# A convolution and spectral mixing kernel: the first row block through another queue, taps and masks on 32 partitions

## Chip, cores and metric

The kernel runs on one core of a Trainium2 chip. A core has TensorE (PE: matrix products, results in PSUM), VectorE (DVE), ScalarE (ACT), GpSimd (POOL) and SyncE (SP), each with its own instruction queue, and 16 DMA engines which carry out the transfers that SP, ACT and POOL issue. The metric is the time of one execution in microseconds (us). The three runs before lie between 171.89 and 172.04, with a median of 171.96.

## What is computed

The input `x` is (8, 3264, 192) in float32: batch, sequence, channels. The first step is a causal convolution along the sequence with 7 taps for each of 8 heads of 24 channels; the taps are a softmax of `weight` (8, 7). The second step works on the result: a Fourier transform along the sequence, of which 64 modes are kept and multiplied by complex 192 x 192 matrices, transformed back and added.

```python
w = np.exp(weight - np.max(weight, axis=-1, keepdims=True))
w = w / (np.sum(w, axis=-1, keepdims=True) + 1e-09)
...
out = np.einsum('hk,bskhg->bshg', w, x_unf)         # causal, 7 taps, group of 24 channels
...
X = np.fft.rfft(x, axis=1)
Xr, Xi = (np.real(X[:, :n_modes]), np.imag(X[:, :n_modes]))
Yr = np.einsum('bmd,mde->bme', Xr, w_r) - np.einsum('bmd,mde->bme', Xi, w_i)
Yi = np.einsum('bmd,mde->bme', Xr, w_i) + np.einsum('bmd,mde->bme', Xi, w_r)
Y[:, :n_modes] = Yr + 1j * Yi
u = x + np.fft.irfft(Y, n=S, axis=1)
return (u + np.maximum(u @ w_ch, 0.0)).astype(np.float32)
```

## The kernel before

The sequence is cut into 13 row blocks of 256 rows (the last has 192), the batches into four pairs. `xall` holds all of `x` in bf16: one partition holds two neighbouring rows (a row pair) of one block, side by side for both batches of a pair. Slot 0 of `xall` is zero, as the past of the first block; of the last block of each pair only 96 partitions are filled by loads, and the other 32 (the tails) are set to zero. The order of the instructions on each engine is that of the program text.

**Loads.** All of `x` comes on POOL's queue (q0), in transfers that read float32 and write bf16. Six units of 5, 8, 9, 10, 10 and 10 blocks (`UNITS`) are loaded by `load_unit`, one transfer for each batch of a pair (L165) and one for the short last block (L169). Behind them, on the same queue, come the 64 mode matrices `moe_w_r` and `moe_w_i` (L296), into `arena` and into the end of `ct`. A new transfer waits until the transfer eight places before it has landed. SP's queue carries only `weight` at the start (L172) and all outputs at the end (L691).

**Band.** The convolution is a product with a band matrix. VectorE builds it: the softmax taps (L224 to L234), four masks (L199) that compare an index `cidx` with 0 to 3, and 14 predicated copies (L242) that put taps into `packed` where a mask holds. Until now this was done on all 128 partitions, with `goff` (L188) and L197 correcting `cidx` in each group of 32. Four small copies for each half of the heads (ScalarE L250, VectorE L252) then bring `packed` into `band`. Before that ScalarE writes zeros into the band (L186) and into the tails (L190).

**Convolution and tables.** TensorE first runs 92 idle matmuls (L196), then convolves unit by unit (L317); ScalarE and VectorE copy the results back into `xall` (L351, L353, L359, L361). The sine and cosine tables are computed beside that (L209 to L221), and the transform along the sequence is a product with them (L378). Between the units, and after them, TensorE transposes `xall` into `ct` (L419).

**Mixing and output.** L551 multiplies four modes at a time, in 16 groups, each with matrices from q0. The last group is followed by the output stage: L723 and L703 form the products of the channel matrix and of the inverse transform, ScalarE clamps (L696), VectorE adds (L685) and SP stores (L691).

The lines of the table builder and the order of the load and the idle matmuls are in the functions printed below.

Of the kernel before, what the change touches and what calls it, by code (L numbers as in the profile page):

```python
# [9 lines left out]
ALU = mybir.AluOpType  # L10
ACT = mybir.ActivationFunctionType
AX = mybir.AxisListType
F32 = mybir.dt.float32
# [7 lines left out]
def kernel(  # L21
# [9 lines left out]
    nc = tc.nc  # L31
    B, S, D = x.shape
    H, KK = weight.shape
# [4 lines left out]
    P = 128  # L38
    NQ = B // 2
    NB = S // (2 * P) + 1  # L40
    NT = 2 * NB
    PL = (S - 2 * P * (NB - 1)) // 2
    NSLOT = NQ * NT + 2
    PW = 32 + KK // 2
# [10 lines left out]
    def sb(name, shape, dtype):  # L55
        return pool.tile([P] + shape, dtype, tag=name, name=name)
# [7 lines left out]
    ct = sb("ct", [NQ * NT * 3, P], BF16)  # L64
# [7 lines left out]
    band = shared[:, 0:H * 2 * BW].rearrange("p (h o c) -> p h o c", h=H, o=2)  # L72
# [7 lines left out]
    ascale = sb("ascale", [1], F32)  # L80
    halfpi = sb("halfpi", [1], F32)
    xs = [sb(f"xs{i}", [2, D], BF16) for i in range(2)]
    xacc = ct[:, 0:6, :].rearrange("p t s -> p (t s)").bitcast(F32)
    ylate = xs[0][:, :, :].rearrange("p i d -> p (i d)")


    xin = xall[:, :, :, :].rearrange("p (b x) i d -> p b (x i d)", x=2)
# [15 lines left out]
    def temp(n, dtype):  # L103
        w = n * 2 if dtype == F32 else n
        a = arena[:, pos[0]:pos[0] + w]
        pos[0] += (w + 15) // 16 * 16
        return a.bitcast(dtype) if dtype != BF16 else a
# [5 lines left out]
    wsub = temp(H * KK, F32)  # L113
    wexp = temp(H * KK, F32)
    taps = temp(H * KK, BF16)
    wmax = temp(H, F32)
    wsum = temp(H, F32)
    wrec = temp(H, F32)
    wsin = temp(H, F32)
    cidx = temp(PW, F32)  # L120
    goff = temp(1, F32)
    masks = temp((KK // 2 + 1) * PW, U16)
    sidx = temp(NT, F32)
    midx = temp(MODES, F32)
# [30 lines left out]
    def load_unit(g0, n):  # L155
        for part in parts_of(g0, n):
            load_part(*part)

    def load_part(q, b0, n):
        nf = min(n, NB - 1 - b0)  # L160
        s0 = NB * q + b0 + 1
        for i in range(2):
            off = ((2 * q + i) * S + 2 * P * b0) * D
            src = bass.AP(tensor=x.tensor, offset=x.offset + off, ap=[[2 * D, P], [2 * P * D, nf], [1, 2 * D]])
            nc.gpsimd.dma_start(out=xin[:, s0:s0 + nf, 2 * D * i:2 * D * (i + 1)], in_=src)  # L165
        if nf < n:
            off = (2 * q * S + 2 * P * (NB - 1)) * D
            src = bass.AP(tensor=x.tensor, offset=x.offset + off, ap=[[2 * D, PL], [S * D, 2], [1, 2 * D]])
            nc.gpsimd.dma_start(out=xin[0:PL, s0 + nf, :].rearrange("p (i c) -> p i c", i=2), in_=src)  # L169

    wr3 = wraw.rearrange("p (h k) -> p h k", h=H)
    nc.sync.dma_start(out=wr3, in_=bass.AP(tensor=weight.tensor, offset=weight.offset,  # L172
                                           ap=[[0, P], [KK, H], [1, KK]]))
    load_unit(*units[0])
    nc.gpsimd.iota(cidx[:, 0:PW], pattern=[[1, PW]], base=0, channel_multiplier=-1,
                   allow_small_or_imprecise_dtypes=True)
    load_unit(*units[1])
    nc.gpsimd.iota(sidx.rearrange("p (b a) -> p b a", a=2), pattern=[[2 * P, NB], [1, 2]], base=0,
                   channel_multiplier=2, allow_small_or_imprecise_dtypes=True)
# [4 lines left out]
    zero = packed[:, 0:2].bitcast(F32)  # L184
    bandrow = shared[:, 0:H * 2 * BW].bitcast(F32)
    nc.scalar.copy(out=bandrow, in_=zero.to_broadcast([P, H * BW]))  # L186
    for g in range(4):
        nc.vector.memset(goff[32 * g:32 * g + 32, :], float(32 * g))  # L188
    tails = xin[PL:P, NB:NB * NQ + 1:NB, :].bitcast(F32)
    nc.scalar.copy(out=tails, in_=zero[PL:P, :].unsqueeze(2).to_broadcast([P - PL, NQ, 2 * D]))  # L190
    nc.vector.memset(halfpi[:], math.pi / 2)
    nc.vector.memset(ascale[:], 2.0 / S)
    nc.vector.memset(ascale[0:2 * B, :], 1.0 / S)
    zeros = xall[:, 0, 0, :]
    for _ in range(NIDLE):
        nc.tensor.matmul(free[3][:, 0, 0:144], zeros[:, 0:P], zeros[:, 0:144], start=True, stop=True, skip_group_check=True)  # L196
    nc.vector.tensor_scalar(out=cidx[:, 0:PW], in0=cidx[:, 0:PW], scalar1=goff[:, 0:1], scalar2=None, op0=ALU.add)  # L197
    for k in range(KK // 2 + 1):
        nc.vector.tensor_scalar(out=masks[:, PW * k:PW * (k + 1)], in0=cidx[:, 0:PW],  # L199
                                scalar1=float(k), scalar2=None, op0=ALU.is_equal)  # L200
    tu3 = turns.rearrange("p (t m) -> p t m", t=NT)
    wh3 = whole.rearrange("p (t m) -> p t m", t=NT)
# [1 line left out]
    def table(step, t0, t1):  # L204
# [15 lines left out]
        else:  # L220
            nc.scalar.activation(out=ftab[:, t0:t1, 0:2 * MODES - 1:2], in_=wh, func=ACT.Sin, scale=-TWOPI,  # L221
                                 bias=halfpi[:, 0:1])

    nc.vector.reduce_max(out=wmax, in_=wr3, axis=AX.X)  # L224
    nc.vector.tensor_tensor(out=wsub.rearrange("p (h k) -> p h k", h=H), in0=wr3,
                            in1=wmax.unsqueeze(2).to_broadcast([P, H, KK]), op=ALU.subtract)
    nc.scalar.activation(out=wexp, in_=wsub, func=ACT.Exp)
    nc.scalar.activation(out=wsin, in_=ascale.to_broadcast([P, H]), func=ACT.Sin)
    we3 = wexp.rearrange("p (h k) -> p h k", h=H)
    nc.vector.reduce_sum(out=wsum, in_=we3, axis=AX.X)  # L230
    nc.vector.tensor_scalar(out=wsum, in0=wsum, scalar1=1e-9, scalar2=None, op0=ALU.add)
    nc.vector.reciprocal(out=wrec, in_=wsum)
    ta3 = taps.rearrange("p (h k) -> p h k", h=H)
    nc.vector.tensor_tensor(out=ta3, in0=we3, in1=wrec.unsqueeze(2).to_broadcast([P, H, KK]), op=ALU.mult)  # L234


    pk4 = packed.rearrange("p (h o c) -> p h o c", h=H, o=2)
    for h0 in (0, H // 2):
        hs = slice(h0, h0 + H // 2)
        for lag in range(KK):  # L240
            k = lag // 2
            nc.vector.copy_predicated(  # L242
                out=pk4[:, hs, lag % 2, :],
                mask=masks[:, PW * k:PW * (k + 1)].unsqueeze(1).to_broadcast([P, H // 2, PW]),
                data=ta3[:, hs, KK - 1 - lag:KK - lag].to_broadcast([P, H // 2, PW]))
        for g in range(4):
            c0 = 1 + 32 * (g % 2)
            dst, srcv = band[32 * g:32 * g + 32, hs, :, c0:c0 + PW], pk4[32 * g:32 * g + 32, hs, :, :]
            if h0 == 0:
                nc.scalar.copy(out=dst, in_=srcv)  # L250
            else:
                nc.vector.tensor_copy(out=dst, in_=srcv)  # L252
# [4 lines left out]
                            base=0, pattern=[[-1, P]], channel_multiplier=1)  # L257
    nc.gpsimd.memset(perm[:], 0.0)
    nc.gpsimd.affine_select(out=perm[:, 0:64], in_=perm[:, 0:64], compare_op=ALU.not_equal, fill=-1.0,
                            base=-64, pattern=[[-1, 64]], channel_multiplier=1)  # L260
    nc.gpsimd.affine_select(out=perm[:, 64:128], in_=perm[:, 64:128], compare_op=ALU.not_equal, fill=1.0,
                            base=0, pattern=[[-1, 64]], channel_multiplier=1)

    for i in range(2):
        nc.gpsimd.memset(apart[i][:], 0.0)
        for c in range(2):
            nc.gpsimd.affine_select(out=apart[i][:, 64 * c:64 * c + 64], in_=apart[i][:, 64 * c:64 * c + 64],
                                    compare_op=ALU.not_equal, fill=-1.0 if (i, c) == (1, 0) else 1.0,
                                    base=-(c ^ i), pattern=[[-2, 64]], channel_multiplier=1)
# [601 lines left out]
```

## Time and profile before

| | |
|---|---|
| median of three runs | 171.96 us |
| the profiled execution, its whole time | 171.92 us |
| its span, first to last instruction | 169.8 us |
| TensorE (matmul) busy | 160.1 us, 94% |
| VectorE busy | 125.7 us, 74% |
| ScalarE busy | 109.8 us, 65% |
| GpSimd busy | 44.3 us, 26% |
| POOL's queue q0 | 19.62 MB |
| SP's queue q1 | 20.09 MB |

The profile shows one execution. Besides the span there are 2.1 us around it. The page gives busy time by engine, then the span in 40 slices of 4.245 us with a digit for the busy tenths of each, then the chain of waits that ended last, followed back from the last instruction, and groups of instructions by line. The trace answers more closely: the chain in order of time, instructions by time (the timeline), and busy time in windows that one names. Lines like L551 are lines of the kernel before; in the changed kernel the same code lies eight lines lower from the convolution on.

### The profile page before, as it was taken

What the parts mean: (1) busy time and instruction counts of PE and PEld (TensorE: products, weight loads), DVE (VectorE), ACT (ScalarE), POOL (GpSimd) and SP (SyncE); (2) the same over time, 40 slices, a digit from 0 to 9 for tenths busy, and PEclk for the clock granted to TensorE, in tenths of its full rate; (3) what the DMA queues carried; (4) which work ended last, traced back from release to release, by engine and by line L of the source; (5) the groups of instructions that cost most, each with busy time, mean ns of one, the idle gap of its engine ahead of it and who ended that gap; (6) DMA issues with size and microseconds to landing.
All of it is one profiled execution on the core that took longest, in us unless ns stands there. A gap on an engine that the chain in (4) does not pass through costs nothing.

```text
span 169.8 us, 6332 instructions
## 1 busy us (share of the span) xinstructions
PE 160.1 (94%) x2643; PEld 129.9 (77%) x2643; DVE 125.7 (74%) x245; ACT 109.8 (65%) x209; POOL 44.3 (26%) x81
## 2 busy tenths in 40 slices
PE   6996999999999999999999889999999999999990
PEld 6983776775655656589999655899899999999960
DVE  4899762883763846568778544899899999999990
ACT  8485870753663627447677554688788888888771
POOL 7941963522521612003520000990000000000000
PEclk9999999999999999999999999999999999999999
DMA  3999999999999999999999970588989989999996
GB/s 28 201 203 203 204 205 203 204 204 204 201 205 204 209 205 208 208 208 208 209 204 209 208 120 4 192 299 321 365 333 346 350 300 358 358 324 339 330 343 221
DMA packets 36956, 40.10 MB, mean 236 GB/s; under 512 B 2272, under 2 KB 36928, under 8 KB 36928
## 3 DMA queue, kind: packets, MB, share of 16 engines
q0 software_dynamic: 22624, 19.62, 72.1%
q1 hardware_dynamic: 14304, 20.09, 32.3%
q8 instruction: 20, 0.33, 0.8%
q14 instruction: 8, 0.07, 0.1%
HBM read 39.10 MB, written 20.05 MB: 348 GB/s over the span
## 4 chain that ended last, share of the span: by engine, by line
DMA 57%; PE 37%; issue 1%; POOL 1%; ACT 1%; POOLq 0%
PE z L723 34%; DMA xall<-in_x_dram 25%; DMA arena<-in_moe_w_i_dram 18%; DMA ct<-in_moe_w_i_dram 14%; PE z L703 1%; POOL xall L165 1%; PE z L644 0%; PE z L551 0%; ACT z L696 0%; ACT arena L683 0%; PE z L635 0%; ACT shared L569 0%; PE z L645 0%; PE z L575 0%; PE z L804 0%
## 5 line engine op out<-in xcount | busy, mean ns | idle before, releaser
L685 DVE TENSOR_TENSOR arena<-z,xall 128x384 f32<-128x384 f32 (+1 forms) x103 | 57.0, 557 | 3.0 <-PE z L723 1.2
L696 ACT ACTIVATE z<-z 128x384 f32<-128x384 f32 x102 | 48.1, 475 | 12.1 <-PE z L723 3.7
L723 PE MATMUL z<-arena,ftab 64*128 64x384 bf16 x308 | 45.6, 323 | 0.1
L723 PEld LDWEIGHTS <-ct 64*128 64x128 bf16 x600 | 42.5, 94 | 1.6 <-issue 0.3
L723 PE MATMUL z<-wsw,ct 64*128 64x192 bf16 x300 | 42.1, 243 | 0.0
L317 PE MATMUL z<-xall,shared 64*64 64x480 bf16 (+3 forms) x768 | 38.8, 338 | 0.6 <-DMA xall<-in_x_dram 0.3
L317 PEld LDWEIGHTS <-shared 64*64 64x64 bf16 x768 | 25.1, 106 | 11.9 <-issue 2.0
L723 PE MATMUL z<-wm,ct 64*128 64x192 bf16 x200 | 34.1, 243 | 0.0
L361 DVE CAST xall<-z 128x480 bf16<-128x480 f32 (+1 forms) x32 | 20.6, 645 | 12.7 <-PE z L317 11.8
L723 PEld LDWEIGHTS <-ftab 64*128 64x128 bf16 x396 | 26.7, 93 | 1.4 <-issue 0.7
L359 ACT CAST xall<-z 128x480 bf16<-128x480 f32 (+1 forms) x32 | 17.5, 548 | 14.6 <-PE z L317 14.6
L723 PE MATMUL z<-w,ct 64*128 64x192 bf16 x100 | 24.3, 243 | 0.0
L416 DVE COPY ct<-z 128x1024 bf16<-128x1024 bf16 x27 | 18.4, 687 | 5.2 <-PE z L419 4.5
L419 PE MATMUL z<-ident,xall 128*128 128x128 bf16 x312 | 20.0, 219 | 0.0
L419 PEld LDWEIGHTS <-xall 128*128 128x128 bf16 x312 | 17.7, 98 | 1.9 <-issue 1.1
L378 PE MATMUL z<-xall,ftab 128*128 128x384 bf16 (+3 forms) x114 | 18.0, 312 | 0.2 <-DVE xall L361 0.2
L165 POOL DMA_DIRECT2D xall<-in_x_dram x16 | 14.3, 901 | 12.2 <-DMA xall<-in_x_dram 11.4
L378 PEld LDWEIGHTS <-ftab 128*128 128x128 bf16 (+1 forms) x114 | 10.2, 98 | 7.6 <-issue 1.5
L414 ACT COPY ct<-z 128x1024 bf16<-128x1024 bf16 x12 | 12.1, 1012 | 4.1 <-PE z L419 4.0
L723 PE MATMUL z<-mixa,ftab 64*128 64x384 bf16 x88 | 13.6, 323 | 0.0
L584 POOL DMA_DIRECT2D arena<-xs x16 | 7.9, 504 | 18.0 <-ACT xs L580 18.0
L296 POOL DMA_DIRECT2D arena<-in_moe_w_r_dram x7 | 4.6, 653 | 20.7 <-PE z L551 14.2
(116 smaller groups left out, 145.9 us busy)
## 6 DMA issues: line engine op xcount, KB each, us to landing
out_dram<-arena SPq DMA_DIRECT2D x47, 384.0 KB, 3.5
xall<-in_x_dram POOLq DMA_DIRECT2D x4, 864.0 KB, 17.4
xall<-in_x_dram POOLq DMA_DIRECT2D x4, 576.0 KB, 18.4
arena<-in_moe_w_r_dram POOLq DMA_DIRECT2D x3, 576.0 KB, 15.4
arena<-in_moe_w_i_dram POOLq DMA_DIRECT2D x3, 576.0 KB, 15.0
ct<-in_moe_w_r_dram POOLq DMA_DIRECT2D x3, 576.0 KB, 20.6
ct<-in_moe_w_i_dram POOLq DMA_DIRECT2D x3, 576.0 KB, 23.5
xall<-in_x_dram POOLq DMA_DIRECT2D x2, 672.0 KB, 11.0
```

The source lines that it names most:

```text
L165: nc.gpsimd.dma_start(out=xin[:, s0:s0 + nf, 2 * D * i:2 * D * (i + 1)], in_=src)
L317: yield nc.tensor.matmul(o, band[r, h, int(a != a1), c0:c0 + 64], xin5[r, s1:s1 + n, :, a1, dsl], start=(row == 0 and a1 == 0), stop=(row ...
L359: nc.scalar.copy(out=dst[:, a], in_=srcv)
L361: nc.vector.tensor_copy(out=dst[:, a], in_=srcv)
L378: nc.tensor.matmul(xp[:, :, ds], ftab[0:k, t, :], xall[0:k, NT * q + t, :, ds], start=(j == 0), stop=(j == len(work) - 1), skip_group_chec ...
L414: nc.scalar.copy(out=out, in_=in_)
L416: nc.vector.tensor_copy(out=out, in_=in_)
L419: nc.tensor.matmul(o, in_, ident[:], start=True, stop=True, is_transpose=True)
L584: nc.gpsimd.dma_start(out=zwl[k:k + 1, :, :, :].rearrange("p b t d -> p b (t d)"), in_=ylate[r + 2:r + B, :])
L685: nc.vector.tensor_tensor(out=o[0:pn, :, a, :], in0=srcv, in1=xall[0:pn, s + a, :, :], op=ALU.add)
L696: nc.scalar.activation(out=z, in_=z, func=ACT.Relu)
L723: mm = nc.tensor.matmul(target(bank[k], cols, r), l, r, start=first, stop=last, skip_group_check=True)
```

## The change

The first row block of the first pair of batches no longer comes with unit 0 on POOL's queue. SP issues eight transfers for it, four for each batch, which bring float32 into `xfull`, a part of `ct` that is unused until later; each takes every fourth row pair, so every fourth partition, 32 rows of 1536 bytes. ScalarE turns the two halves of `xfull` into bf16 in `xall`. Unit 0's transfers on POOL's queue have four blocks instead of five.

Index, masks, softmax, taps and predicated copies work on partitions 0 to 31 only, and all four groups of `band` are copied from there; `goff` and L197 are gone, and `weight` is loaded for 32 partitions. The softmax's first half and the Sin that loads ScalarE's table move ahead of the masks. The tails are zeroed by two VectorE memsets instead of one ScalarE copy.

```diff
+    xfull = ct[:, 80:92, :].rearrange("p t s -> p (t s)").bitcast(F32)
...
         for i in range(2):
-            off = ((2 * q + i) * S + 2 * P * b0) * D
-            src = bass.AP(tensor=x.tensor, offset=x.offset + off, ap=[[2 * D, P], [2 * P * D, nf], [1, 2 * D]])
-            nc.gpsimd.dma_start(out=xin[:, s0:s0 + nf, 2 * D * i:2 * D * (i + 1)], in_=src)
+            o = int((q, b0) == (0, 0))
+            off = ((2 * q + i) * S + 2 * P * (b0 + o)) * D
+            src = bass.AP(tensor=x.tensor, offset=x.offset + off, ap=[[2 * D, P], [2 * P * D, nf - o], [1, 2 * D]])
+            nc.gpsimd.dma_start(out=xin[:, s0 + o:s0 + nf, 2 * D * i:2 * D * (i + 1)], in_=src)
...
-    nc.sync.dma_start(out=wr3, in_=bass.AP(tensor=weight.tensor, offset=weight.offset,
-                                           ap=[[0, P], [KK, H], [1, KK]]))
+    nc.sync.dma_start(out=wr3[0:32], in_=bass.AP(tensor=weight.tensor, offset=weight.offset,
+                                                 ap=[[0, 32], [KK, H], [1, KK]]))
+    for i in range(2):
+        for r in range(4):
+            nc.sync.dma_start(out=xfull[r:P:4, 2 * D * i:2 * D * (i + 1)],
+                              in_=bass.AP(tensor=x.tensor, offset=x.offset + (i * S + 2 * r) * D,
+                                          ap=[[8 * D, P // 4], [1, 2 * D]]))
...
-    for g in range(4):
-        nc.vector.memset(goff[32 * g:32 * g + 32, :], float(32 * g))
-    tails = xin[PL:P, NB:NB * NQ + 1:NB, :].bitcast(F32)
-    nc.scalar.copy(out=tails, in_=zero[PL:P, :].unsqueeze(2).to_broadcast([P - PL, NQ, 2 * D]))
...
+    nc.vector.memset(xin[PL:P, NB:NB * NQ // 2 + 1:NB, :], 0.0)
...
-    nc.vector.tensor_scalar(out=cidx[:, 0:PW], in0=cidx[:, 0:PW], scalar1=goff[:, 0:1], scalar2=None, op0=ALU.add)
+    lo = slice(0, 32)
+    nc.vector.reduce_max(out=wmax[lo], in_=wr3[lo], axis=AX.X)
+    nc.vector.tensor_tensor(out=wsub[lo].rearrange("p (h k) -> p h k", h=H), in0=wr3[lo],
+                            in1=wmax[lo].unsqueeze(2).to_broadcast([32, H, KK]), op=ALU.subtract)
+    nc.scalar.activation(out=wexp[lo], in_=wsub[lo], func=ACT.Exp)
+    nc.scalar.activation(out=wsin, in_=ascale.to_broadcast([P, H]), func=ACT.Sin)
+    nc.vector.memset(xin[PL:P, NB * (NQ // 2 + 1):NB * NQ + 1:NB, :], 0.0)
+    for i in range(2):
+        nc.scalar.copy(out=xin[:, 1, 2 * D * i:2 * D * (i + 1)], in_=xfull[:, 2 * D * i:2 * D * (i + 1)])
     for k in range(KK // 2 + 1):
-        nc.vector.tensor_scalar(out=masks[:, PW * k:PW * (k + 1)], in0=cidx[:, 0:PW],
+        nc.vector.tensor_scalar(out=masks[lo, PW * k:PW * (k + 1)], in0=cidx[lo, :],
                                 scalar1=float(k), scalar2=None, op0=ALU.is_equal)
...
             nc.vector.copy_predicated(
-                out=pk4[:, hs, lag % 2, :],
-                mask=masks[:, PW * k:PW * (k + 1)].unsqueeze(1).to_broadcast([P, H // 2, PW]),
-                data=ta3[:, hs, KK - 1 - lag:KK - lag].to_broadcast([P, H // 2, PW]))
+                out=pk4[lo, hs, lag % 2, :],
+                mask=masks[lo, PW * k:PW * (k + 1)].unsqueeze(1).to_broadcast([32, H // 2, PW]),
+                data=ta3[lo, hs, KK - 1 - lag:KK - lag].to_broadcast([32, H // 2, PW]))
...
-            dst, srcv = band[32 * g:32 * g + 32, hs, :, c0:c0 + PW], pk4[32 * g:32 * g + 32, hs, :, :]
+            dst, srcv = band[32 * g:32 * g + 32, hs, :, c0:c0 + PW], pk4[lo, hs, :, :]
```

The rest of the softmax (sum, reciprocal, product) stays behind the table's function, on 32 partitions.

More of the change, by code (lines that the diff above doesn't have):

```diff
@@ L120 @@
     cidx = temp(PW, F32)
-    goff = temp(1, F32)
     masks = temp((KK // 2 + 1) * PW, U16)
@@ L171 @@
     wr3 = wraw.rearrange("p (h k) -> p h k", h=H)
-    nc.sync.dma_start(out=wr3, in_=bass.AP(tensor=weight.tensor, offset=weight.offset,
-                                           ap=[[0, P], [KK, H], [1, KK]]))
+    nc.sync.dma_start(out=wr3[0:32], in_=bass.AP(tensor=weight.tensor, offset=weight.offset,
[5 more added lines that the diff above has]
+                                          ap=[[8 * D, P // 4], [1, 2 * D]]))
     load_unit(*units[0])
-    nc.gpsimd.iota(cidx[:, 0:PW], pattern=[[1, PW]], base=0, channel_multiplier=-1,
+    nc.gpsimd.iota(cidx[0:32, :], pattern=[[1, PW]], base=0, channel_multiplier=-1,
                    allow_small_or_imprecise_dtypes=True)
@@ L222, in table @@
                                  bias=halfpi[:, 0:1])
[L224 to L228, printed above, removed]
     we3 = wexp.rearrange("p (h k) -> p h k", h=H)
-    nc.vector.reduce_sum(out=wsum, in_=we3, axis=AX.X)
-    nc.vector.tensor_scalar(out=wsum, in0=wsum, scalar1=1e-9, scalar2=None, op0=ALU.add)
-    nc.vector.reciprocal(out=wrec, in_=wsum)
+    nc.vector.reduce_sum(out=wsum[lo], in_=we3[lo], axis=AX.X)
+    nc.vector.tensor_scalar(out=wsum[lo], in0=wsum[lo], scalar1=1e-9, scalar2=None, op0=ALU.add)
+    nc.vector.reciprocal(out=wrec[lo], in_=wsum[lo])
     ta3 = taps.rearrange("p (h k) -> p h k", h=H)
-    nc.vector.tensor_tensor(out=ta3, in0=we3, in1=wrec.unsqueeze(2).to_broadcast([P, H, KK]), op=ALU.mult)
+    nc.vector.tensor_tensor(out=ta3[lo], in0=we3[lo], in1=wrec[lo].unsqueeze(2).to_broadcast([32, H, KK]), op=ALU.mult)
     pk4 = packed.rearrange("p (h o c) -> p h o c", h=H, o=2)
```

## The prediction

> **What bounds the kernel now.** I read the page's slices first, then the chain of waits in order of time, the waits by engine, and last the timeline and narrow windows of the two places where the change acts: the first 10 us, and the end of the loads near 100 us. The slices:
>
> ```profile
> PE   6996999999999999999999889999999999999990
> DMA  3999999999999999999999970588989989999996
> GB/s 28 201 203 203 204 205 203 204 204 204 201 205 204 209 205 208 208 208 208 209 204 209 208 120 4 192 299 321 365 333 346 350 300 358 358 324 339 330 343 221
> ```
>
> From the second slice to the 23rd (4.2 us to 97.6 us) the DMA engines are full at 201 to 209 GB/s: bytes as written, in bf16; what is read is float32, twice as much, some 406 GB/s. All of that is q0, the GpSimd queue. The chain of waits agrees (start, length, what):
>
> ```profile
> 3.37 9.62 DMA xall<-in_x_dram
> ...
> 13.27 19.59 DMA xall<-in_x_dram
> ...
> 87.84 13.91 DMA arena<-in_moe_w_i_dram
> 101.75 0.04 issue
> 101.80 0.49 PE z L551 x12
> ...
> 106.66 51.07 PE z L723 x714
> ```
>
> Until 101.75 us the end is set by when q0 has moved its bytes; behind it comes TensorE work without a hole. But TensorE is nearly dense before 101.75 as well, so I ask how much it waits for those loads:
>
> ```profile
> PE z L551 <- DMA arena<-in_moe_w_i_dram: 1.0, 2, 0.6
> ...
> PE z L317 <- DMA xall<-in_x_dram: 0.3, 1, 0.3
> ```
>
> The two waits of L551 stand in the timeline at 96.07 (0.42 us) and at 101.80 (0.56 us). So TensorE, with no late load, would be at L551 of the last group 0.98 us sooner. That is the ceiling: the output stage begins at the later of "q0 done" (now 101.75) and "TensorE done with all else" (now about 100.8).
>
> **What q0 loses.** One row block of two batches: 2 x 128 rows x 384 values, 196.6 KB in bf16, 393.2 KB as read. At 203.5 GB/s, the rate of slices 1 to 9, that is 0.97 us less on q0. A saturated queue passes this on whole: POOL's waits for landings (11.4 us at L165) move with it, since up to eight transfers are always outstanding.
>
> **What SP's queue gains.** The same 393.2 KB, as eight transfers of 48 KB. Where engines are full with q0 each costs 393.2/8 KB at 407 GB/s read, 0.12 us; all eight 0.97 us, exactly what was removed. So the gain is only what gets through before q0 fills the engines. That moment is seen in narrow windows (last two columns: DMA share as a mean over the 16 engines, GB/s):
>
> ```profile
> 2.60:2.80 0.20, 0.20 (x5) 0.20 (x2) 0.00 (x0) 0.20 (x1) 0.20 (x1) 1.00 0.08 19
> 2.80:3.00 0.20, 0.20 (x4) 0.20 (x3) 0.00 (x0) 0.20 (x1) 0.20 (x1) 1.00 0.33 20
> ...
> 3.70:3.80 0.10, 0.10 (x4) 0.10 (x2) 0.10 (x1) 0.10 (x1) 0.10 (x1) 1.00 0.46 23
> ...
> 4.10:4.20 0.10, 0.10 (x3) 0.10 (x2) 0.10 (x1) 0.10 (x1) 0.10 (x1) 1.00 0.92 138
> 4.20:4.30 0.10, 0.10 (x4) 0.10 (x2) 0.10 (x1) 0.10 (x1) 0.10 (x1) 1.00 1.28 200
> ```
>
> Up to 4.2 us the engines are mostly free. SP issues the weights at 0.74 us for 0.38; an issue on SP has a median of 0.37 us (the 53 of L691). So the eight issues start at 1.12, 1.49 ... 3.71 us. When their data move is not shown by any row, so I bound it. Soonest: the first output transfer is issued at 106.80 and its data show from 107.55, 0.75 us later; so the eight begin between 1.9 and 4.5 us, six of them before 4.2 have gone, two contend (0.24 us): a gain of 0.73. Latest: the weights, the first transfer on this queue, are issued at 0.74 and the DMA share rises only near 2.85, 2.1 us later; so the eight begin between 3.2 and 5.8, three are through, five contend (0.60 us): 0.37. The output row is nearer in packet size (1536 B here and there), the weight row nearer in time; neither is clearly the nearest, and I take the middle, 0.55 us.
>
> [...]
>
> **The first POOL issue.** Its two transfers have four blocks instead of five. Issues on L165 take 0.76 us for three blocks, 0.83 for six, 1.0 for nine: some 0.04 a block, so q0 may start up to 0.08 us sooner. I take 0.05.
>
> **The weights.** 32 partitions instead of 128: a quarter of the 1024 small packets that keep the DMA share near 1 from 3.0 to 3.5 us. Whether q0 could have run there isn't shown; bounds are nothing and 0.3 us (from 3.4 to 4.2 us the engines ramp up at 23 to 138 GB/s). I take nothing, the ramp being far below full without weights too.
>
> **VectorE before the band.** Going from 128 to 32 partitions shortens no instruction: the 32x280 copies and the 128x280 memset both go by columns (0.23 and 0.29 us). Removed: four goff memsets (0.37 together) and L197 (0.84). Added: two tail memsets of 768 words, at the 1 ns a word of L182 and L183 (280 in 0.29, 384 in 0.38) 0.77 us each. The first falls into the hole of 1.40 us before 3.50 and is free. The softmax's first half now goes ahead of the masks; it needs the weights, which landed at 3.64 and may land as soon as 2.8 (issue at 0.74 plus the 2.0 us of the shortest output). The second memset overlaps ScalarE's Exp. From there: masks some 0.7 to 0.9, then reduce, add, reciprocal and multiply as before (5.86 to 6.79, 0.93), so the first copy_predicated starts between 6.1 and 7.0 us; now 6.79. From both sides: -0.7 to +0.2 us.
>
> **ScalarE before the band.** The tail copy goes (1.47 us at 3.11). Exp, table load and Sin keep their 1.77 us (5.58 to 7.35) but start near 4.0 to 4.5, so they end by 5.7 to 6.3. Then two casts of 128x384 at 0.48 (the row of L381). They wait for the eight transfers, the last landing near 5.7 to 6.6 (issue at 3.71 plus the 2.0 us of the shortest output or the 2.9 of the weights). Casts over by 7.3 at the latest; the band copies queued behind them need seven predicated copies, 1.66 us, so 7.8 to 8.7. They hide the casts by half a microsecond or more; without that cover the casts cost at most 0.96 us at the band.
>
> **TensorE's start.** The 92 idle matmuls end at 9.34; convolution starts at 9.68, after q0's first landing. Unit 0 is a fifth shorter on q0, so its landing comes 0.37 to 0.73 sooner, and convolution starts between 9.34 and 9.6. So TensorE's side does not get later, and 0.98 us of room is enough for the gain.
>
> **Sum.** 0.55 + 0.05 = 0.60 us off "q0 done": L551 of the last group at 101.2 instead of 101.80, all behind it rigid. Span 169.2 instead of 169.8, profiled time 171.3 instead of 171.92. The profiled run stands 0.04 us under the median, 171.96; from that, 171.4.
>
> **Rivals.**
> First, no gain: the transfers contend with q0 all the same. SP's first transfer of data may start late, as the weights' did, or the eight may keep q0 from ramping up, each 48 KB taking the engines from packets that would have gone. For it: share 0.9 to 1.7 at 3.0 to 3.5 us with only 28 KB moving. Against: idle engines before 2.8 us. Gain 0 to 0.3: 171.65 to 171.95. [...]
>
> Second, slower: the band comes late. ScalarE's band copies now stand behind casts that wait for all eight transfers. TensorE has 0.98 us of room, and the copies start at 8.48 now; so the end moves back only if they start later than 9.46, that is, if the last transfer lands after 9.0 (the first cast can be done before). Each microsecond beyond that is one on the end: landing at 9.7 would give 172.65. Against it: 53 output transfers, up to 384 KB, landed in 2.0 to 5.1 us, and 3.71 + 5.1 is 8.8. [...]
>
> Third, more than forecast: nearly all eight get through free, and fewer weight packets let q0 start up to 0.3 us sooner. Gain 0.9 to 1.2, against a ceiling of 0.98 plus what TensorE starts sooner (0.1 to 0.3): near 170.9.
>
> **How the numbers follow.** 0.2% of 171.96 is 0.34 us, about what can be told from no change. Forecast (gain 0.35 to 0.85): 0.56. No gain: 0.24. Slower: 0.12. More: 0.08. Faster is 0.56 + 0.08 = 0.64, same 0.24, slower 0.12. The range takes in forecast and no-gain with the run-to-run spread, and most of the third: 170.95 to 172.15; the slower rival stays outside. The forecast's own range is 171.1 to 171.6.
>
> **What would show it.** Right: q0 0.2 MB smaller; in narrow windows more than 60 GB/s before 3.4 us that isn't q0's; full load from about 4.2 as now; the last landing of the chain at 101.1 to 101.4; waits of L551 for DMA down from 0.98 to about 0.4 us. Wrong if the last landing stays at 101.6 or later (first rival), if those waits vanish while L551 comes later (second), or if the DMA is full well before 4.2 us.

## The result and the profile after

The changed kernel is slower: 173.52 us in the median of six runs (172.68 to 173.98), against 172.11 for the kernel before beside it. The ratio is 1.0065, 95% interval 1.0044 to 1.0087. Ratios leave out the slow runs, those over 1.5% above the fastest of their kernel (one with two late transfers, one with two row blocks), and they are not quotients of the medians. The profiled execution took 173.95 us, its span is 171.6.

The slices of the page after, TensorE, the granted clock and the DMA engines:

```profile
PE   6949999999999999999999999999999999999990
...
PEclk9996999999999999999999999999999999999999
DMA  3999999999999999999999930389999989999995
```

Two digits are new: TensorE is idle for more than half of the third slice (8.6 to 12.9 us), and the clock granted to it in the fourth is below full. The DMA row starts as before.

The chain of waits in order of time (start, length, what) no longer consists of DMA pieces. It now runs through ScalarE's band copies and TensorE:

```profile
12.10 0.43 ACT shared L258
...
13.46 5.13 PE z L325 x87
...
103.95 0.42 PE z L559 x11
```

So q0 no longer sets the start of the output stage; the beginning of the convolution does. L559 is the L551 of before; the last group's first product stands at 103.88, before at 101.80. ScalarE's timeline shows who held the band:

```profile
4.67 0.21 ACT L207 ACTIVATE arena<-ascale 128x8 f32<-128x8 f32 x1
8.54 0.51 ACT L210 CAST xall<-ct 128x384 bf16<-128x384 f32 x1 [3.66 <-DMA ct<-in_x_dram]
11.24 0.51 ACT L210 CAST xall<-ct 128x384 bf16<-128x384 f32 x1 [2.19 <-DMA ct<-in_x_dram]
11.66 1.75 ACT L258 COPY shared<-arena 32x280 bf16<-32x280 bf16 x4
```

ScalarE waits 5.85 us in all for the eight transfers, and the band copies behind the casts start at 11.66 instead of 8.48. The eight transfers by their source line (durations of the issue in ns, first and last start, then issue to landing):

```profile
L179 SPq DMA_DIRECT2D ct<-in_x_dram x8: 543/594/656, 1.2 to 5.7; - x8
...
DMA to landing us min/median/max: 2.0/5.2/5.6
```

TensorE's timeline from 9 us, and two windows of the clock (the third column from the right is the granted clock). First the same stretch in the kernel before, with its band copies:

```profile
8.48 1.75 ACT L250 COPY shared<-arena 32x280 bf16<-32x280 bf16 x4 [1.14 <-DVE arena L242]
9.68 4.29 PE L317 MATMUL z<-xall,shared 64*64 64x240 bf16 x128 [0.34 <-DMA xall<-in_x_dram]
16.05 0.60 PE L455 MATMUL z<-shared 128*128 128x512 bf16 x2 [1.54 <-issue]
16.49 1.14 PE L378 MATMUL z<-xall,ftab 128*128 128x384 bf16 x6
```

Now the changed kernel:

```profile
8.82 1.29 PE L201 MATMUL z<-xall 128*128 128x144 bf16 x18
12.57 6.02 PE L325 MATMUL z<-xall,shared 64*64 64x240 bf16 x128 [2.47 <-ACT shared L258]
18.52 1.04 PE L463 MATMUL z<-shared 128*128 128x512 bf16 x4
19.57 0.66 PE L386 MATMUL z<-xall,ftab 128*128 128x384 bf16 x3
```
```profile
14.00:17.00 3.00, 3.00 (x68) 2.94 (x64) 0.00 (x0) 2.08 (x4) 0.00 (x0) 0.50 1.31 200
17.50:18.60 1.10, 1.10 (x33) 0.92 (x26) 0.66 (x1) 1.10 (x3) 1.02 (x4) 1.00 1.32 205
```

Between these two profiles the sum closes. Convolution starts 2.89 us later (12.57 against 9.68). Unit 0 takes 6.02 instead of 4.29 us, 1.73 more. In the kernel before a hole of 1.54 us followed unit 0, between the second and third of four L455 products; it is gone. What it waits for is not shown: the trace names no releaser ("issue"), and the kernel with two transfers and 80 idle matmuls, below, has no such hole though its convolution starts at 9.73. That the late start closed it is therefore argued, not shown. 2.89 + 1.73 - 1.54 = 3.08, and the next step, L378 (now L386), starts 3.08 later (19.57 against 16.49). TensorE's room of 0.98 us near 100 us swallows a part, which leaves 2.10; measured at the last group: 2.08. The output stage, from there to the last ScalarE copy, was 0.43 us shorter in this profile, counted from start to start (63.28 against 63.71). Why is open, but it is not chance: it takes 63.28 to 63.34 us in the profiles of all ten kernels of this document that have the new load code together with the rest of the change, the one without the bytes included, and 63.69 to 63.71 in those of the four others (the kernel before, both with the loads back, and the one with the load part alone).

### The profile page after: what moved, and what is told of

The parts are those of the page before. It is cut to its first block, busy times and chain, and to the rows that moved or that the text cites. A ratio compares the mean times of both kernels' runs of the same rounds, so it can differ in the third digit from the quotient of the medians.

```text
span 171.6 us, 6360 instructions
## 1 busy us (share of the span) xinstructions
PE 162.1 (94%) x2643; PEld 128.7 (75%) x2643; DVE 126.6 (74%) x242; ACT 110.0 (64%) x210; POOL 45.6 (27%) x81
## 2 busy tenths in 40 slices
DMA packets 36988, 40.27 MB, mean 235 GB/s; under 512 B 2304, under 2 KB 36960, under 8 KB 36960
## 4 chain that ended last, share of the span: by engine, by line
PE 85%; ACT 3%; DVE 2%; issue 1%; DVEq 0%; ACTq 0%
PE z L731 34%; PE z L325 20%; PE z L427 12%; PE z L386 10%; PE z L559 3%; PE z L661 1%; PE z L404 1%; PE z L711 1%; ACT xall L359 1%; DVE ct L424 1%; ACT shared L258 1%; PE z L643 1%; ACT ftab L234 1%; PE z L463 1%; DVE xall L361 1%
## 5 line engine op out<-in xcount | busy, mean ns | idle before, releaser
L731 PE MATMUL z<-arena,ftab 64*128 64x384 bf16 x308 | 44.9, 322 | 0.0
L325 PE MATMUL z<-xall,shared 64*64 64x480 bf16 (+3 forms) x768 | 40.3, 350 | 2.9 <-ACT shared L258 2.5
L325 PEld LDWEIGHTS <-shared 64*64 64x64 bf16 x768 | 26.3, 112 | 14.4 <-ACT shared L258 3.0
L731 PE MATMUL z<-wsw,ct 64*128 64x192 bf16 x300 | 35.1, 243 | 0.0
L731 PEld LDWEIGHTS <-ftab 64*128 64x128 bf16 x396 | 29.8, 93 | 2.5 <-PE z L731 0.2
L731 PE MATMUL z<-wm,ct 64*128 64x192 bf16 x200 | 29.9, 243 | 0.0
L386 PE MATMUL z<-xall,ftab 128*128 128x384 bf16 (+3 forms) x114 | 18.1, 312 | 0.2 <-DVE xall L369 0.2
L386 PEld LDWEIGHTS <-ftab 128*128 128x128 bf16 (+1 forms) x114 | 10.2, 98 | 8.0 <-issue 1.5
```

The costliest lines, as they stand in the source:

```text
L325: yield nc.tensor.matmul(o, band[r, h, int(a != a1), c0:c0 + 64], xin5[r, s1:s1 + n, :, a1, dsl], start=(row == 0 and a1 == 0), stop=(row ...
L386: nc.tensor.matmul(xp[:, :, ds], ftab[0:k, t, :], xall[0:k, NT * q + t, :, ds], start=(j == 0), stop=(j == len(work) - 1), skip_group_chec ...
L731: mm = nc.tensor.matmul(target(bank[k], cols, r), l, r, start=first, stop=last, skip_group_check=True)
```

## Experiments

All ratios are to the kernel before on the same chip, with 95% intervals.

**Which part of the change?** First the change without its load part:

```diff
-            o = int((q, b0) == (0, 0))        # five blocks on POOL's queue again
...
-    for i in range(2):                        # no eight transfers on SP
-        for r in range(4):
-            nc.sync.dma_start(out=xfull[r:P:4, ...
...
-        nc.scalar.copy(out=xin[:, 1, ...], in_=xfull[...])
```

> The changed kernel with its first row block back on POOL's queue (no transfers on SP but the weights, no casts); band on 32 partitions and tails as changed. Theory A (the wait for the eight transfers, which land at 11.2 us, holds the band copies and so the convolution): the loss is gone, convolution starts between 9.34 and 9.7 us, time within 0.3 us of before, 171.7 to 172.3. Theory B (the loss is in VectorE's and ScalarE's new order, the tails or the band on 32 partitions): the time stays 1 us or more above before, 173 to 174.

Measured: 171.74 us, ratio 0.9960 (0.9944 to 0.9977). Convolution starts at 9.42. So everything else in the change (weights, masks, taps, tails) costs nothing, and even gains a little. A repetition, below, confirms that.

Then the load part alone, the same lines added to the kernel before:

> The kernel before with only the load part of the change: eight transfers on SP, two casts ahead of the band copies, four blocks on POOL's queue; weights, masks, goff and tails as before. Theory A: the whole loss is here, convolution starts at 12 us or later, 173.2 to 174.2. Theory B: 171.4 to 172.1.

Measured: 173.68 us, ratio 1.0087 (1.0064 to 1.0110). Convolution starts at 12.75, unit 0 takes 5.91. Theory A holds and B falls: the loss is in the load part.

**The wait or the traffic?** The transfers stay, but nothing early waits for them:

```diff
-        nc.scalar.copy(out=xin[:, 1, 2 * D * i:2 * D * (i + 1)], in_=xfull[:, 2 * D * i:2 * D * (i + 1)])
+        nc.scalar.copy(out=xin[:, 1, 2 * D * i:2 * D * (i + 1)], in_=xin[:, 0, 2 * D * i:2 * D * (i + 1)])
```

> The changed kernel, all transfers in place, but the two casts read the zero slot of xall instead of what the transfers bring, so that nothing early waits for them (the first row block counts as zero). Theory A: convolution starts at 9.4 us, TensorE is again ahead of q0 near 100 us, and what is left is the relief of q0 alone: 171.0 to 171.8, a gain over before of 0.2 to 0.9. Theory C (the eight transfers take as much from q0 as they relieve it of): 171.8 to 172.2. Theory B: 173 or more.

Measured: 171.01 us, ratio 0.9926 (0.9912 to 0.9940), all six runs between 170.90 and 171.09. Convolution starts at 9.35 with the same eight transfers in flight. Waiting for them is what costs. With the wait gone the kernel is faster than the one with its loads back.

The counterpart leaves the eight transfers out as well, so that nobody loads the first row block:

> As the kernel in which nothing waits for the eight transfers (the casts read the zero slot), but the eight transfers are left out altogether: the first row block is loaded by nobody and counts as zero. Its distance to the kernel with the loads back on POOL's queue is the whole worth of taking 0.97 us of bytes off q0; its distance to the kernel with the transfers in place is what they cost by contention. If bytes of q0 set the end one for one: 0.9 to 1.0 us under the kernel with loads back (about 170.8), and 0.3 or more under the kernel with transfers in place (171.01). If TensorE's room or the end of the queue swallow most of it: 171.0 to 171.5.

> The kernel with its loads back on POOL's queue once more, unchanged, as the partner on the same chip: 171.5 to 171.9 again if its gain over before holds, 172.0 to 172.3 if the first measurement was chance.

Measured on one chip: 170.26 us without the bytes (0.9888, 0.9864 to 0.9912) and 171.59 with loads back on POOL's queue (0.9962, 0.9950 to 0.9973). Three medians stand in order: bytes on q0 171.59 (171.74 the first time), bytes on SP without a wait 171.01, no bytes 170.26. The steps are 0.58 us (0.73 against the first measurement) and 0.75; the intervals of the last two only touch (at 0.9912).

These differences are not q0's alone. The output stage is shorter by 0.41 us in both kernels without a wait. It does not follow the bytes, since it is short with and without them, and 0.41 of the 0.58 and of the 1.33 us between the first and the last go with it. The end of q0 shows directly, loads back first, then the transfers on SP without a wait:

```profile
87.58 14.12 DMA arena<-in_moe_w_i_dram
...
101.74 0.46 PE L550 MATMUL z<-arena,mixa 128*16 128x192 bf16 x12 [0.55 <-DMA arena<-in_moe_w_i_dram]
```
```profile
87.58 14.02 DMA arena<-in_moe_w_i_dram
...
101.64 0.46 PE L559 MATMUL z<-arena,mixa 128*16 128x192 bf16 x12 [0.55 <-DMA arena<-in_moe_w_i_dram]
```

q0's last landing stands at 101.70 and 101.60; without the bytes it is at 100.7 (issued at 87.0, 13.7 us to landing). So taking the block off q0 is worth 1.0 us at that point, what its 0.97 us of bytes come to, and bringing it by eight transfers on SP gives 0.9 of that back: 0.1 remains. Theory C thus falls for the time but nearly holds for q0. These are single profiles, and that of the kernel without the bytes is the slowest of its six runs (171.07). Of the 0.58 that the medians differ by, 0.17 are left for q0 and the end of the kernel together.

**What sets the landing?** The same block in two transfers of 128 partitions:

```diff
-        for r in range(4):
-            nc.sync.dma_start(out=xfull[r:P:4, 2 * D * i:2 * D * (i + 1)], ...
-                                          ap=[[8 * D, P // 4], [1, 2 * D]]))
+        nc.sync.dma_start(out=xfull[:, 2 * D * i:2 * D * (i + 1)], ...
+                          in_=bass.AP(..., ap=[[2 * D, P], [1, 2 * D]]))
```

> The changed kernel with two transfers of 128 partitions (192 KB each) on SP in place of eight of 32. Theory A with the landing set by the moment of issue (a transfer issued before q0 fills the engines lands in 2 to 4 us, one issued later takes 5): issues at 1.2 and 1.8 us, landings by 6.5, casts over by 7.1, convolution from 9.4, 171.0 to 171.8, faster than before. Rival D (landing set by the bytes that SP's queue brings beside q0, whatever their number of transfers): last landing near 10 to 11 us again, 173 to 174.

Measured: 171.53 us, ratio 0.9959 (0.9938 to 0.9981). Issues of 0.41 to 0.43 us at 1.18 and 1.65; landings 2.5 and 3.3 us later. ScalarE's timeline has no wait before the casts:

```profile
4.67 0.21 ACT L205 ACTIVATE arena<-ascale 128x8 f32<-128x8 f32 x1
4.78 0.91 ACT L208 CAST xall<-ct 128x384 bf16<-128x384 f32 x2
7.21 1.75 ACT L256 COPY shared<-arena 32x280 bf16<-32x280 bf16 x4 [1.52 <-DVE arena L248]
```

In its profile the last group's product stands at 101.20, 0.60 us sooner than before. Rival D falls: the same bytes land by 5 us. Still open was whether the moment of issue or the number of transfers decides. Two transfers held back on SP until q0 is in full flow tell that apart:

```diff
+    nc.vector.memset(xfull[:, 0:1], 0.0)             # behind the second tail memset
+    nc.vector.memset(xfull[:, 2 * D:2 * D + 1], 0.0)
+    (the two transfers here)
```

> Two transfers as in the kernel with two, but SP holds each back until VectorE has written a word of its target, behind the second tail memset, so that they are issued at about 4.1 and 4.6 us, when q0 has filled the engines. Theory T (turns): each needs only a few turns, landing 2 to 3.5 us after issue, by 8 us; convolution at 9.4 to 10. Theory A (moment of issue): 5 us or more after issue as for the late ones of eight, landing at 9.5 to 10, convolution from about 11.

Measured: 173.09 us, ratio 1.0074 (1.0048 to 1.0099). Issued at 4.12 and some 0.4 later, they land 5.6 and 6.3 us after issue:

```profile
9.80 0.51 ACT L210 CAST xall<-ct 128x384 bf16<-128x384 f32 x1 [4.92 <-DMA ct<-in_x_dram]
10.92 0.51 ACT L210 CAST xall<-ct 128x384 bf16<-128x384 f32 x1 [0.61 <-DMA ct<-in_x_dram]
```

So the moment of issue decides here, not the number: theory T falls. Its turns, and the 1 us of q0's for a small packet, were a conjecture of mine that no run shows. In the changed kernel q0 has filled the engines by 4.1 us (184 to 219 GB/s from 4.1 to 4.8); what SP issued after that landed 5.3 to 5.6 us after issue there (three of 48 KB), close to the 5.6 and 6.3 of the two of 192 KB here. The border lies earlier than that, though. Transfers issued by 1.7 us landed 1.7 to 4.0 us later in the changed kernel and its variants; of the eight in the changed kernel the second, issued at 1.78, already took 4.1, and yet its DMA windows show only 0 to 77 GB/s from 3.3 to 3.8 us. What holds the transfers back before the engines are full is not shown.

This profile tells of the landing, not of the loss. It is of the fastest of the eight runs (171.81, clock 0.995, unit 0 in 4.62 us); the others had a granted clock of 0.980 to 0.989.

Does the step of four partitions matter? Eight transfers of neighbouring partitions:

```diff
-            nc.sync.dma_start(out=xfull[r:P:4, 2 * D * i:2 * D * (i + 1)], ...
+            nc.sync.dma_start(out=xfull[32 * r:32 * r + 32, 2 * D * i:2 * D * (i + 1)], ...
```

> Eight transfers of 32 neighbouring partitions each in place of every fourth partition. Theory T and theory A: as the changed kernel, last landing 10.5 to 11.5 us, 173 to 174. Rival E (the step of four makes the issue 0.6 us instead of 0.37 and the landing slow): issues of 0.4 us, last landing by 8, 171 to 172.

Measured: 171.54 us (170.91 to 173.13), ratio 0.9974 (0.9943 to 1.0005). The eight issues take 3.82 us instead of 5.15 (a median of 0.42 each, with short gaps, instead of 0.59), and the last lands 4.9 us after its issue, near 9.5 (the second cast starts at 9.49). That is between the cases: the step makes each issue some 0.17 us longer, and the eighth starts over a microsecond later for it (5.70 against 4.56). Rival E's landing by 8 us did not come.

**How much is the clock?** More idle matmuls, so that TensorE does not pause:

```diff
-    NIDLE = 92
+    NIDLE = 142
```

> The changed kernel with 142 idle matmuls instead of 92, so that TensorE works through its pause from 10.1 to 12.6 us (the idle matmuls take 0.05 us each by then). If the half clock granted from 13.9 to 17.1 us comes from that pause, unit 0's convolution takes 4.3 us again instead of 6.0 and the last group's L559 comes 1.4 to 1.7 us sooner: 172.1 to 172.7. If the half clock has another cause, or the room at the end hides it: 173.2 to 174.

Measured: 171.99 us, ratio 0.9997 (0.9978 to 1.0015), though the second cast still starts at 11.31. TensorE's timeline and the granted clock in the window that was at half before:

```profile
7.82 5.04 PE L201 MATMUL z<-xall 128*128 128x144 bf16 x78
12.79 4.48 PE L325 MATMUL z<-xall,shared 64*64 64x240 bf16 x128
```
```profile
14.00:17.00 3.00, 3.00 (x107) 2.60 (x96) 0.50 (x1) 2.78 (x7) 0.10 (x1) 1.00 1.31 202
```

Convolution starts even later than in the changed kernel, yet the last group's product is at 102.17 instead of 103.88. So in these profiles the pause costs 1.7 us at that point (unit 0 alone 1.5: 6.02 against 4.48), and the late start puts it 0.37 us behind the kernel before. In the medians the pause is worth less: 1.2 us by the ratios, 1.5 by the medians themselves (the profiled execution here, 171.66, is the fastest of twelve).

That the time is that of the kernel before does not make the late start free. The kernel in which nothing waits has the same transfers and an early start, and it is at 0.9926: against that the late start still costs 1.0 us by the medians, 1.2 by the ratios. The loss of some 2.4 us against that kernel is thus about half late start and half clock.

**Versions that might beat both.** One transfer for the whole block:

> The changed kernel with one transfer for the whole first row block (128 partitions, both batches, 384 KB) on SP. Theory A (moment of issue) and theory T (each transfer takes its turns with q0 at the engines, one small packet of it for about 1 us of q0's, so the number of transfers sets the landing) agree: issue at 1.2 us, landing by 5, casts hidden, time like the kernel with two transfers, 171.0 to 171.8. Rival D (bytes set the landing): later than 9 us.

Measured: 171.93 us, ratio 0.9991 (0.9973 to 1.0008). The casts start at 4.78 as with two, but convolution waits 0.55 us for q0's landing and starts at 10.66. No gain.

Two row blocks by two transfers (POOL's unit 0 has three blocks):

> Two transfers on SP, each with the first two row blocks of one batch (384 KB), POOL's unit 0 with three blocks. If what gets through before q0 fills the engines (4.2 us) sets the gain: q0 loses another 0.97 us and some half of the added bytes contend, so the last landing comes 0.3 to 0.5 us before that of the kernel with two transfers of one block (101.2), at 100.7 to 100.9, and the time is 170.9 to 171.5. If the second transfer lands beyond 8 us, or the bytes all contend: 171.5 to 172.5.

Measured: 171.64 us, ratio 0.9962 (0.9944 to 0.9980). The transfers land 3.1 and 4.0 us after issue, but in its profile q0's last landing is at 101.99, not at 100.7 to 100.9: twice the bytes bring no more.

Two transfers of one block and 80 idle matmuls:

> The kernel with two transfers of one block, with 80 idle matmuls instead of 92, so that they end before q0's first landing also where TensorE's clock rises late. If the scatter of that kernel (170.6 to 172.2) comes from the end of the idle matmuls (9.35 to 10.1 us), it narrows to 170.8 to 171.6; if it comes from elsewhere, the spread stays over 1 us, or TensorE's clock drops more often in the pause and it is slower.

Measured: 171.47 us (171.07 to 171.96), ratio 0.9952 (0.9933 to 0.9971). The lowest median of those that compute everything, 0.5% under the kernel before and 1.1% under the changed one by the ratios, but not separable from the kernel with its loads back on POOL's queue (0.9962). The runs span 0.9 us where those with 92 idle matmuls span 1.6, but six runs against ten do not show a narrower spread. The highest, 171.96, is outside the range that was expected of it. Why two early transfers do not reach the 171.01 of the kernel in which nothing waits stays open. In the profile with 92 idle matmuls q0's last landing (101.2) and the last ScalarE copy (164.48 against 164.92) come sooner than there, yet the execution took 171.35 against 170.90. With one transfer, two row blocks or 80 idle matmuls q0's last landing is at 102.0 to 102.2, later than in the kernel before.

## Why the prediction was wrong

The bound was read rightly: where TensorE is not late, q0's last landing still releases the last group. Two steps failed.

The step that made the kernel slower is "ScalarE before the band": the last landing "near 5.7 to 6.6" came at 11.2. Two terms were too small. The issues: 0.37 us each, from the outputs; measured 0.54 to 0.66, so the eighth starts at 5.7 instead of 3.71. And the landing: 2.0 to 2.9 us, from the shortest output and the weights; only the first of the eight had that (2.0), the next took 4.1, the other six 4.8 to 5.6. The rows for a loaded queue were on the page: q0's own transfers, with medians of 11 to 24 us from issue to landing in most of their groups; I had read that as depth of that queue alone.

The gain failed as well ("What SP's queue gains", 0.55 us). It counted three to six of the eight transfers as through before 4.2 us; in the changed kernel only the first had landed by then (at 3.2), and the second came at 5.9. Contention was priced at 0.24 to 0.60 us; it took back 0.9 at q0's end, so that 0.1 remained of the forecast 0.60. The 0.97 for the bytes themselves was right (1.0). The medians differ by 0.58 to 0.73, which looks like the forecast, but that is luck: 0.41 of it is the output stage, a term that the prediction did not have.

The second rival named the mechanism and its place, and gave it 0.12. Its price of the wait, one for one past 9.0, would be 174.15 for a landing at 11.2; the profiled run took 173.95. That agreement is partly luck: the rival left out the clock (most of the 1.73 us by which unit 0 is longer) and the hole of 1.54 us that is gone. With the clock held, the last group's product came 0.37 us late, not 2.2. What was missing in the prediction is thus also a term, put at nothing: what TensorE's pause costs beyond its length. The list of what would show the forecast wrong had the pattern that came: no DMA wait at L559, and L559 later. The first rival's sign came too, q0's last landing at 101.7 (issued at 87.8, 13.9 us to landing), but here the last issues had waited for a late TensorE, so it can't tell the two apart.

The first rival, no gain by contention, fell as a time (0.9926 with all transfers in place) but not as a mechanism: a gain of 0.1 us at q0's end lies in its 0 to 0.3. Of the 1.0 us that q0 was spared, 0.9 came back in these profiles.

VectorE's part was right in kind (the 14 predicated copies take 3.08 us on 32 partitions, 3.10 on 128) and too cautious in size: the first copy_predicated starts at 5.53, ahead of the 6.1 to 7.0 given, since the tail memsets took 0.70, the weights landed at 2.4 and the masks needed 0.43. "TensorE's start" assumed that the idle matmuls end at 9.34; in this run they ended at 10.1, because the fast half of them (10 to 12 in half a microsecond, 7 until then) began near 7.1 us instead of 5.4. One row was misread without harm to the sum: the DMA share near 1 from 3.0 to 3.5 us, put down to the weights' small packets, is in the changed kernel too (1.97 and 2.20 from 3.0 to 3.2 us), where the weights had landed at 2.4. Nor does a quarter of 1024 packets show: those under 512 B are 2272 before and 2304 after.

The change without its load part is 0.4% faster than before (0.9960 and 0.9962), which the prediction had at nothing. In its trace the band copies start at 7.43 instead of 8.48, while the last group's product stays at 101.74; where the 0.4 us are saved was not settled.

## What to carry to other kernels

A transfer that is moved to an idle queue is only as early as its issue (the eighth here was issued at 5.7 and landed at 11.2). What mattered here is whether it was issued in the first 1.7 us, well before the other queue filled the DMA engines at 4.1 (x landed 2.0 to 4.0 us after such an issue, in the changed kernel 4.8 to 5.6 after one from 2.4 us on): so few large transfers at the very start, not many small ones. Price a landing beside a full queue from rows taken under load, and count who queues behind the instruction that waits for it. Where a wait makes TensorE pause, add what the clock does after the pause (in the changed kernel 3.4 us at half clock, 1.5 us more for unit 0); here idle matmuls across the pause took away the loss against the kernel before, but not the half of the wait's cost that the late start makes. And before a difference of medians is put down to the term that was changed, look in the profiles for where it arises: 0.41 us of the gain here lay in a stage that the bytes do not touch.

## What the runs showed of the hardware

A pause of TensorE of 2.47 us was followed, a good microsecond after work resumed, by half clock from about 13.8 to 17.2 us, some 3.4 us. In the kernel with the load part alone 3.4 us of half clock followed a pause of 2.88. A pause of 1.83 us brought the same 3.4 us in the kernel with eight transfers of neighbouring partitions (unit 0 in 5.96 us), but a pause of 1.83 us in the one with two late transfers did not (full clock, unit 0 in 4.62 us). So the pause's length alone does not decide, and what else does is not shown.

Issues of x on SP's queue took 0.36 to 0.48 us for 128 partitions, 0.41 to 0.55 for 32 neighbouring ones, and 0.54 to 0.66 for 32 with a step of four in the changed kernel.
